# A planned order of 780 tasks, made anew: the combined weight w1·wo ahead of the first products of x, and the weight differences on VectorE alone

## The chip, the cores and the metric

The kernel runs on one core of one Trainium2 chip. The metric is the device time of one execution in microseconds (us). Five engines share the work: TensorE (PE in the profile, with PEld for its weight loads), VectorE (DVE), ScalarE (ACT), GpSimd (POOL) and SyncE (SP), which here issues nearly all DMAs. Each engine takes its instructions strictly in the order in which they are written, and waits where an input isn't there.

## The reference

```python
# q, k, v: (4, 8, 768, 64) float32; block 32, window 16, nb = 24
k_sum = k.reshape(B, H, nb, block, D).max(axis=3)
v_sum = v.reshape(B, H, nb, block, D).mean(axis=3)
scores_l = scale * q @ k^T,  kept where |i - j| < 16
scores_s = scale * q @ k_sum^T + log(block)
a = softmax(concat(scores_l, scores_s))
attn = a @ concat(v, v_sum)
x = attn.transpose(0, 2, 1, 3).reshape(3072, 512)
out = maximum(x @ w1, x @ w2) @ w_out      # w1, w2: (512, 1024), w_out: (1024, 512)
```

A local attention with block summaries is followed by a two-way maximum layer and an output product.

## The kernel before

The kernel uses max(x·w1, x·w2) = x·w1 + relu(x·(w2 - w1)). So it never forms x·w1: it multiplies w1·wo once into a 512x512 matrix (names w1o), and the output is x·w1o + relu(x·wd)·wo with wd = w2 - w1. Everything is computed in bf16 with float32 sums.

**Tiles.** The four batches are done one after the other. In each batch the 8 heads make 4 head pairs (hp 0 to 3), and the 768 rows make 3 groups of 256 (grp 0 to 2). Names carry these: k02 is the k block of batch 0, head pair 2; exp 021 is batch 0, head pairs 2 and 3, group 1; hidden 013 is batch 0, group 1, quarter 3.

**Steps of a batch.** k, q and v blocks (393 KB each) land in one of 13 float32 buffers (land), are cast to bf16 (kqb, vx), k and q are turned by PE (L624) or, in some late blocks, by a DMA transpose, and placed (kx, qx). For each pair of head pairs and each group PE makes the scores (L701), ACT the exponential (L715), DVE masks (L725, batches 1 to 3), PE multiplies with v and the block means (L757), DVE divides (L813, L816) into xs. xs is turned into xt by PE (L831, batch 0) or by a DMA transpose (L822, the other batches). Then follow four hidden products per group (L913, "hidden") with a relu each (L922 on ACT, L924 on DVE), and two output blocks (L940 with w1o, L947 with wo), copied and stored (L958).

**Weights.** w1 and w2 come as four tiles each (w0 to w3 in the plan's names), 0.52 MB, wo as four tiles as well. From each pair of tiles wd n = w2 - w1 is made (L856). The w1 tile is cast (w1b), turned by PE (L869, "turn w1") and copied out of PSUM (w1t). w1o takes 8 half blocks of 4 products on PE (L897): the first half of a block needs wo 0 and wo 1, the second wo 2 and wo 3. Their copies are the w1o tiles. Because a land buffer is freed only when its readers are done, a weight tile's buffer stays taken until both its cast and its wd are through.

**What sets the order.** The program is a list of 780 tasks, each with inputs, outputs and a choice of engines. Three tables fix the rest: `order` (in which order tasks are issued, hence each engine's queue), `engines` (a letter per task with a choice: T, D, A, P, S for PE, DVE, ACT, POOL, SP) and `slots` (which buffer of a ring each result takes).

```python
def given(self, order, slots):
    for t in order:
        for b in self.tasks[t].new:
            if b.slot is None:
                b.take(slots.pop(0))
        self.tasks[t].fn(self.tasks[t].letter)
```

Of the kernel before, what the change touches and what calls it, by code (L numbers as in the profile page):

```python
# [22 lines left out]
CFG = dict(  # L23
    kc="DAPA", qc="AAAA", kp="DDDD", qp="AADA", tl="DDDD", od="DDDD", se="AAAA", sr="PPPP", vc="PPPP",
    wd="PDDD", w1b="PPAD", w1t="DADD", wo="AADD", xt="AADDDD", kv=0.2, sp=0.7, ones=1, on="DDD", w=(30,
    31, 32, 33, 50, 51, 52, 53, 200, 201, 202, 203), wt=25, g0=(10, 30, 210), g1=(20, 30, 40), w1o=450, mx=1500,
    woc=600, wdp=30, lk="ADDP", lq="AAPA", lod="DPS", lse="DDD", lsr="DDP", lvc="DPPPDDAPPAPA", ltl="DDPD", ld=500, warm=14, cold=16500,
    turn="22 23 30 31 32 33", lx="SSS", cols=True, emb=1, ep=0.5, vt=0.28, s32=0.36, raw=0, qg=0, wh=1, os=6,
)
CFG["order"] = list(map(int, """  # L30
# [26 lines left out]
""".split()))  # L57
CFG["engines"] = "".join("""
PDPPPDDDPAPDPDDDDPTTTTTTTTTTTTTTSSSAAAATDDPPSSSADPATAAPPSSSPDDPTADDDSSSPDDPTADDPSSDPTASSPATDSSDATDSSPATASDSASASDDTDTAD
PPPDDTDTADPDADDTATDDPDDDPTATDDPPDDTTATDDTDTTATDDTDTTATDDTDTTATDDTDTTATDDTATTATDDTDSSSPSSSPSSSDSSSPPADAPDDDTAPDPAAPDPAT  # L60
DTDDADDDPTATDDPADDTADTDDSTADTDDSTADTDDSATPTADADADDTDTDDADAATADTDDSTADTDDSTADTDDSSSSPSSSASSSASSSPPDAPDDPPTDPPPAAAPPATDT
ADPAAAATPTADPPPDTADTDDSTADTDDSTADTDDSPSPSDDPAAASASDDPPPTADTDDSTADTDDSTADTDDSSSSPSSSPSSSASSSPPDAPDDPDTAPADPPPPPASPSDDAD
PDSDSDDPPDTADTDDSTADTDDSTADTDDSASPSADAADPSDSADAPDTADTDDSTADTDDSTADTDDSTTATTATTDTTDTDTATDTATTTDSTTTDSTATATATATTTAATTTAS
TATATDTDTTTASTTTDSTDTATDTDTTTDATTTDSTDTATATDTTTDATTTASTATDTATATTTDSTTTDSTATDTATATTTDATTTAATDTATATATTTASTTTASTATATATATT
TDSTTTAATDTDTDTDTTTDSTTTDATDTATDTDTTTDATTTASTATDTDTATTTAATTTDSTTTDSTTTAA
""".split())
CFG["slots"] = list(map(int, """
# [11 lines left out]
""".split()))  # L79
ENG = {"T": "PE", "D": "DVE", "A": "ACT", "P": "POOL", "S": "SP"}  # L80

# [153 lines left out]
def kernel(  # L235
# [15 lines left out]
    B, H, S, D = 4, 8, 768, 64  # L251
# [11 lines left out]
    op = plan.op  # L263
# [36 lines left out]
    wd = [Buf(Ring([wd_tile[:, n]])) for n in range(4)]  # L300
# [284 lines left out]
    def copy(engine, us, aps, label, port=True, by_engine=False, **kw):  # L585


        def fn(e):
            o, i = aps(e) if by_engine else aps()
            if e == "S":  # L590
                nc.sync.dma_start(out=o, in_=i)
            else:
                {"D": nc.vector.tensor_copy, "A": nc.scalar.copy, "P": nc.gpsimd.tensor_copy}[e](out=o, in_=i)  # L593

        op(engine, us, fn, label=label, port=port, **kw)

    def on(e):
        return {"D": nc.vector, "P": nc.gpsimd}[e]

    def prep(b, hp, prio, k_on, q_on, kp, qp, tail_on):  # L600
# [3 lines left out]
        for n, eng in enumerate((k_on,) if CFG["qg"] and b == 0 else (k_on, q_on)):  # L604
            by_dma = f"{b}{hp}" in CFG["turn"]
# [3 lines left out]
            def cast(e, f=f, src=src, n=n):  # L609
# [3 lines left out]
                if by_dma:  # L613
# [2 lines left out]
                return (src.ap[:].rearrange("p (i h d j) -> p h i j d", h=2, d=D, j=2),  # L616
                        landed(f, 2, J * D).rearrange("p h (i j d) -> p h i j d", d=D, j=2))

            copy(eng, {"D": 0.58, "A": 0.84 if by_dma else 1.06, "P": 0.83 if by_dma else 1.05}, cast, by_engine=True,
                 read=[f], write=[src], prio=prio, label=f"cast {'kq'[n]}{tag}")  # L620

            def turn(src=src, ps=ps):
# [223 lines left out]
    def load_w12(n, prios, prio, prio_t):  # L846
        rows, fs = n // 2, []
        h = half_of[n] // 2
        for w, at in zip((moe_w1, moe_w2), prios):
# [3 lines left out]
                out=landed(f, 2, 512), in_=w.rearrange("(c p) n -> p c n", p=128)[  # L853
                    :, 2 * rows:2 * rows + 2, 512 * h:512 * h + 512]),
               write=[f], prio=at, label=f"load w{n}")
        op(CFG["wd"][n], {"D": 1.23, "P": 2.35}, lambda e: on(e).tensor_tensor(  # L856
            out=wd_tile[:, 2 * h:2 * h + 2, 2 * rows:2 * rows + 2].rearrange("p n c f -> p c n f"),
            in0=landed(fs[1], 2, 512).rearrange("p c (n f) -> p c n f", f=256),
            in1=landed(fs[0], 2, 512).rearrange("p c (n f) -> p c n f", f=256), op=ALU.subtract),
# [145 lines left out]
    for n in range(4):  # L1005
        load_w12(n, CFG["w"][2 * n:2 * n + 2], CFG["wdp"] + 10 * n, CFG["wt"])
# [53 lines left out]
```

## Time and profile before

| | |
|---|---|
| median of 3 runs | 166.0 us (164.26 to 168.96) |
| the profiled execution | 166.2 us, of it 164.4 us span |
| TensorE busy | 153.0 us, 93% of the span |
| VectorE, ScalarE, GpSimd busy | 113.0, 92.9, 57.8 us |
| DMA | 36.46 MB, mean 222 GB/s |
| granted TensorE clock | 1.00 |

Rows of the profile name the line (L913), the engine, the operation, what it writes and reads (out<-in), how many instructions (x384), the busy time and the mean in ns of one, and the idle time before them with what ended it. A row of the timeline begins with the start and the length in us.

### The profile page before, as it was taken

What the parts mean: (1) busy time and instruction counts of PE and PEld (TensorE: products, weight loads), DVE (VectorE), ACT (ScalarE), POOL (GpSimd) and SP (SyncE); (2) the same over time, 40 slices, a digit from 0 to 9 for tenths busy, and PEclk for the clock granted to TensorE, in tenths of its full rate; (3) what the DMA queues carried; (4) which work ended last, traced back from release to release, by engine and by line L of the source; (5) the groups of instructions that cost most, each with busy time, mean ns of one, the idle gap of its engine ahead of it and who ended that gap; (6) DMA issues with size and microseconds to landing.
All of it is one profiled execution on the core that took longest, in us unless ns stands there. A gap on an engine that the chain in (4) does not pass through costs nothing.

```text
span 164.4 us, 4431 instructions
## 1 busy us (share of the span) xinstructions
PE 153.0 (93%) x1793; PEld 100.2 (61%) x1812; DVE 113.0 (69%) x224; ACT 92.9 (57%) x134; POOL 57.8 (35%) x91
## 2 busy tenths in 40 slices
PE   5889978999999999999999999999899999999992
PEld 2346657998565644575687646678545467766651
DVE  3698898579856899994989986569746654163221
ACT  3469995794577698836996645283937312012010
POOL 6058757302242385534672546034630000000000
PEclk9999999999999999999999999999999999999999
DMA  5999999999999999999979997997999996311015
GB/s 157 289 331 303 273 386 383 383 382 371 274 190 289 271 233 219 130 232 136 201 169 229 228 209 162 121 261 150 220 245 335 319 174 167 58 64 70 0 66 189
DMA packets 67700, 36.46 MB, mean 222 GB/s; under 512 B 54624, under 2 KB 61664, under 8 KB 67680
## 3 DMA queue, kind: packets, MB, share of 16 engines
q1 hardware_dynamic: 66208, 33.76, 87.6%
q10 hardware_dynamic: 1472, 2.43, 4.4%
q8 instruction: 14, 0.23, 0.6%
q14 instruction: 6, 0.05, 0.1%
HBM read 25.17 MB, written 6.29 MB: 191 GB/s over the span
## 4 chain that ended last, share of the span: by engine, by line
PE 62%; DMA 14%; DVE 11%; issue 4%; SPq 4%; ACT 2%; POOL 1%; ACTq 0%; POOLq 0%; DVEq 0%
PE banks L913 19%; PE banks L947 17%; PE banks L940 10%; DMA land<-in_k_dram 8%; DMA out_dram<-o 6%; PE banks L897 4%; PE banks L624 3%; PE banks L757 3%; DVE vx L593 3%; PE banks L701 2%; PE banks L982 2%; DVE ks L650 2%; DVE pb L725 2%; DVE kqb L593 1%; SPq L428 1%
## 5 line engine op out<-in xcount | busy, mean ns | idle before, releaser
L913 PE MATMUL banks<-xt,wd 128*128 128x256 bf16 x384 | 45.9, 273 | 0.1
L947 PE MATMUL banks<-wo,g 128*128 128x512 bf16 (+2 forms) x194 | 43.4, 362 | 1.8 <-issue 1.6
L913 PEld LDWEIGHTS <-wd 128*128 128x128 bf16 x384 | 37.3, 98 | 7.8 <-issue 0.5
L947 PEld LDWEIGHTS <-g 128*128 128x128 bf16 x208 | 18.7, 98 | 17.3
L715 ACT ACTIVATE pb<-banks 128x1024 bf16<-128x1024 f32 x24 | 23.6, 1026 | 6.2 <-PE banks L701 3.8
L940 PE MATMUL banks<-w1o,xt 128*128 128x512 bf16 (+2 forms) x100 | 23.5, 362 | 0.2
L922 ACT ACTIVATE g<-banks 128x512 bf16<-128x512 f32 x27 | 15.2, 604 | 7.6 <-PE banks L913 7.6
L924 DVE TENSOR_SCALAR g<-banks 128x512 bf16<-128x512 f32 x21 | 14.1, 686 | 7.8 <-PE banks L913 7.6
L816 DVE TENSOR_TENSOR xs<-banks,inv 128x512 bf16<-128x512 f32 x24 | 16.0, 686 | 4.9 <-DMA xt<-xs 4.4
L593 POOL COPY vx<-sums 32x792 bf16<-32x792 bf16 x15 | 14.7, 983 | 12.5 <-ACT sums L593 7.0
L725 DVE TENSOR_TENSOR pb<-pb,mask 128x1024 bf16<-128x1024 bf16 (+1 forms) x24 | 16.4, 710 | 4.0 <-ACT pb L715 3.7
L593 ACT COPY o<-banks 128x512 f32<-128x512 f32 (+1 forms) x8 | 4.4, 546 | 25.6 <-PE banks L947 21.1
L593 POOL CAST kqb<-land 128x768 bf16<-128x768 f32 x9 | 8.9, 985 | 20.1 <-DMA land<-in_q_dram 9.8
L940 PEld LDWEIGHTS <-xt 128*128 128x128 bf16 x104 | 9.9, 98 | 9.4
L650 DVE TENSOR_REDUCE ks<-kx 128x24 bf16<-128x768 bf16 x16 | 15.0, 945 | 0.2
L593 DVE COPY o<-banks 128x512 f32<-128x512 f32 (+2 forms) x10 | 6.2, 621 | 10.2 <-PE banks L947 8.7
L593 POOL CAST vx<-land 128x768 bf16<-128x768 f32 x10 | 8.9, 889 | 10.2 <-DMA land<-in_v_dram 10.2
L593 ACT CAST kqb<-land 128x768 bf16<-128x768 f32 x11 | 10.3, 943 | 3.2 <-DMA land<-in_k_dram 2.5
L593 DVE CAST kqb<-land 128x768 bf16<-128x768 f32 x12 | 7.0, 590 | 7.1 <-DMA land<-in_k_dram 4.7
L624 PE MATMUL banks<-ident,kqb 128*128 128x128 f32 x60 | 9.7, 278 | 1.4 <-DVE kqb L593 1.1
L757 PEld LDWEIGHTS <-pb 128*64 128x64 bf16 (+1 forms) x384 | 8.0, 110 | 4.9 <-issue 2.8
L757 PE MATMUL banks<-vx,pb 128*64 128x65 bf16 (+1 forms) x384 | 9.5, 196 | 1.3 <-DVE xs L816 0.8
(87 smaller groups left out, 183.1 us busy)
## 6 DMA issues: line engine op xcount, KB each, us to landing
land<-in_k_dram SPq DMA_DIRECT2D x16, 384.0 KB, 6.0
land<-in_v_dram SPq DMA_DIRECT2D x16, 384.0 KB, 6.9
land<-in_q_dram SPq DMA_DIRECT2D x16, 384.0 KB, 5.9
land<-in_moe_w_dram SPq DMA_DIRECT2D x8, 512.0 KB, 9.6
land<-in_moe_w_out_dram SPq DMA_DIRECT2D x4, 512.0 KB, 10.0
out_dram<-o SPq DMA_DIRECT2D x7, 256.0 KB, 4.0
out_dram<-o ACTq DMA_DIRECT2D x4, 256.0 KB, 2.8
out_dram<-w1t SPq DMA_DIRECT2D x3, 256.0 KB, 3.4
```

What stands on the lines that cost most here:

```text
L593: {"D": nc.vector.tensor_copy, "A": nc.scalar.copy, "P": nc.gpsimd.tensor_copy}[e](out=o, in_=i)
L624: nc.tensor.transpose(out=bank(ps)[:, 128 * j:128 * j + 128], in_=src.ap[:].bitcast(F32)[:, 128 * j:128 * j + 128], identity=ident32[:])
L650: op("D", 0.95, lambda e: nc.vector.tensor_reduce(out=ks.ap[:, 0:nb], in_=free(kt(), 128, [256, NM], [192, 2], [32, 2], [1, 32]), axis=AX. ...
L715: op("A", {"A": 1.03}, lambda e: nc.scalar.activation(out=spread(pb.ap[:, 0, 0:1], [192, 8], [128, 2], [1, 64]) if PW > 128 else spread(pb ...
L725: nc.vector.tensor_tensor(out=o, in0=o, in1=spread(mask[:, 2 * u:2 * u + 1, 0:1], [0, n], [64, 2], [1, 64]), op=ALU.mult)
L757: nc.tensor.matmul(out=o, lhsT=p[r], rhs=vx[b].ap[r, par, hp + n, 2 * grp + u, a, 0:D + 1], start=(PW == 128 or par == 0), stop=(last and ...
L816: op("D", 0.69, lambda e: nc.vector.tensor_tensor(out=x.ap[:].rearrange("p n u a d -> p n (u a) d"), in0=spread(bank_tile[:, ps.ap, 0:1], ...
L913: nc.tensor.matmul(out=bank(ps)[:, 256 * s:256 * s + 256], lhsT=wd_tile[:, quarter, c, 128 * s:128 * s + 128], rhs=x.ap[:, c, :], start=(c ...
L922: nc.scalar.activation(out=o, in_=bank(ps), func=ACT.Relu)
L924: nc.vector.tensor_scalar_max(out=o, in0=bank(ps), scalar1=0.0)
L940: nc.tensor.matmul(out=bank(ps, c1 - c0), lhsT=x.ap[:, c, sl], rhs=w1o[c].ap[:, cols], start=(c == 0), stop=False)
L947: nc.tensor.matmul(out=bank(ps, c1 - c0), lhsT=g.ap[:, f, sl], rhs=wo[f // 2].ap[:, f % 2, cols], start=False, stop=(f == FC - 1))
```

## The change

Three things change. The three tables are replaced by others: `order`, `engines` and `slots`. The task wd loses its choice of engine, so all four run on DVE, where before wd 1 and wd 3 ran on POOL. And the planner's cost of an ACT cast of k and q goes from 1.06 to 1.0, a number that a fixed order does not read.

```diff
 CFG["order"] = list(map(int, """
-44 32 2 0 3 10 12 1 4 6 11 15 13 8 112 20 30 26 56 25 46 113 116 9 122 7 123 126 14 47 16 117 34 118 132 168 28 23 133
...
+2 32 112 10 15 44 122 18 26 113 24 34 3 16 123 21 68 56 46 116 70 45 4 1 9 126 128 117 6 7 35 142 132 127 12 118 119 8
...
-            copy(eng, {"D": 0.58, "A": 0.84 if by_dma else 1.06, "P": 0.83 if by_dma else 1.05}, cast, by_engine=True,
+            copy(eng, {"D": 0.58, "A": 0.84 if by_dma else 1.0, "P": 0.83 if by_dma else 1.05}, cast, by_engine=True,
...
-        op(CFG["wd"][n], {"D": 1.23, "P": 2.35}, lambda e: on(e).tensor_tensor(
+        op("D", {"D": 1.23}, lambda e: on(e).tensor_tensor(
```

PE keeps its 239 tasks. DVE has 213 tasks instead of 210, ACT 156 instead of 143, POOL 71 instead of 82, SP 101 instead of 106. Five stores move from SP's queue to ACT's.

**SP, the loads from the 14th on.** in_moe_w rows are halves of a pair of w1 and w2 tiles (512 KB), in_moe_w_out rows are wo. The first twelve loads were all of batch 0; in the new order the first thirteen hold these and one k block of batch 1 (k12). Before:

```order
L852 DMA land_62<-in_moe_w_dram 128x2x512
L852 DMA land_63<-in_moe_w_dram 128x2x512
L852 DMA land_64<-in_moe_w_dram 128x2x512
L428 DMA land_66<-in_k_dram 128x2x384
L852 DMA land_67<-in_moe_w_dram 128x2x512
L852 DMA land_68<-in_moe_w_dram 128x2x512
L428 DMA land_69<-in_k_dram 128x2x384
L852 DMA land_71<-in_moe_w_dram 128x2x512
L852 DMA land_72<-in_moe_w_dram 128x2x512
L883 DMA land_73<-in_moe_w_out_dram 128x2x512
L428 DMA land_70<-in_k_dram 128x2x384
L428 DMA land_74<-in_k_dram 128x2x384
```

Now:

```order
L852 DMA land_70<-in_moe_w_dram 128x2x512
L428 DMA land_62<-in_k_dram 128x2x384
L852 DMA land_63<-in_moe_w_dram 128x2x512
L852 DMA land_67<-in_moe_w_dram 128x2x512
L883 DMA land_68<-in_moe_w_out_dram 128x2x512
L883 DMA land_71<-in_moe_w_out_dram 128x2x512
L883 DMA land_72<-in_moe_w_out_dram 128x2x512
L852 DMA land_64<-in_moe_w_dram 128x2x512
L883 DMA land_66<-in_moe_w_out_dram 128x2x512
L852 DMA land_73<-in_moe_w_dram 128x2x512
L852 DMA land_69<-in_moe_w_dram 128x2x512
L428 DMA land_74<-in_k_dram 128x2x384
```

Before, each tile's w1 and w2 came one behind the other and wo as the 23rd and 26th to 28th load. Now the four w1 tiles are the 14th, 16th, 17th and 21st load (w1, w3, w2, w0), wo 1, wo 0, wo 2 and wo 3 the 18th, 19th, 20th and 22nd, and the w2 tiles, which only wd reads, the 23rd, 24th, 26th and 27th. The first twelve change as well: q00 was the 8th load behind two v blocks, and is the 9th behind three.

**PE, the start of the big blocks.** Before, behind the last turn of xs and the turn of a k block, PE begins hidden (L913):

```order
L831 LDWEIGHTS xs_109
L831 MATMUL banks<-identity,xs_109 128x128
L624 MATMUL banks<-ident_139,kqb_75 128x128 x3
L913 LDWEIGHTS wd
L913 MATMUL banks<-xt_113,wd 128x256
```

Now, behind a turn of xs (x 022), it begins w1o (L897):

```order
L831 LDWEIGHTS xs_110
L831 MATMUL banks<-identity,xs_110 128x128
L897 LDWEIGHTS w1t_125
L897 MATMUL banks<-wo_130,w1t_125 128x512
L897 LDWEIGHTS w1t_125
```

Seven of the eight halves of w1o, the last turn of w1 and three turns of xs now stand between there and the first hidden; before, the eight halves came behind eleven hidden blocks. wo_130 is wo 0.

**DVE, from the second-last group's division to wd.** Before, DVE did two of the four wd behind the first relu (g):

```order
L593 COPY w1t_125<-banks 128x4x256
L924 TENSOR_SCALAR g_120<-banks 128x512
L856 TENSOR_TENSOR wd<-land_71,land_68 128x2x2x256
L856 TENSOR_TENSOR wd<-land_72,land_67 128x2x2x256
L593 COPY kx_80<-banks 128x6x2x64
```

Now the casts of wo 0 and w1b 0 stand among the divisions, and wd 1 and wd 3 ahead of any relu:

```order
L593 CAST wo_130<-land_71 128x1024
L593 COPY kx_80<-banks 128x6x2x64
L813 RECIPROCAL inv_143<-banks 128x8
L816 TENSOR_TENSOR xs_110<-banks,inv_143 128x512
L593 COPY xt_114<-banks 128x512
L593 CAST w1b_123<-land_64 128x1024
L816 TENSOR_TENSOR xs_111<-banks,inv_143 128x512
L650 TENSOR_REDUCE ks_100<-kx_79 128x24
L593 COPY xt_115<-banks 128x512
L856 TENSOR_TENSOR wd<-land_73,land_70 128x2x2x256
L856 TENSOR_TENSOR wd<-land_69,land_63 128x2x2x256
```

(A second RECIPROCAL row, ahead of the w1b cast, is left out.) Behind them follow a maximum of k (L650), a relu, a small copy, and wd 0 and wd 2. On POOL, the casts of wo 2, wo 3, a w1 tile and blocks of k and q of batch 1 stand where its two wd stood. On ACT, the last three exponentials of batch 0 now come behind the cast of a w1 tile and of a k block, and the copies of q from PSUM, which DVE did, are ahead of the first.

More of the change, by code (lines that the diff above doesn't have):

```diff
@@ L30 @@
 CFG["order"] = list(map(int, """
[26 rows of a table removed]
[26 rows of a table added]
 """.split()))
 CFG["engines"] = "".join("""
[L59 to L65, printed above, removed]
+DDDDDPPPPDPDDPDPDPTTTTTTTTTTTTTTSSSPAPPTDDDDSSSDPAATADDDSSSADPATAAPPSSSDADATADDDSSDDTASSDATDSSDPTASSDPTDSDSASPSPDTDTAD
+AADADTPTDDAAAAPTDTDDPDDDATDTDDPPDDTTATDDTATTATDDTDTTATDDTATTATDDTATTATDDTDTTATDDTDSSSPSSSDSSSPSSSPDDDPPDPPTDDAPADPDPPT
+DTDDDPDDPTPTADAPDATADTDDSTADTDDSTADTDDSATPTDDPADDPTDTDDADDDTADTDDSTADTDDSTADTDDSSSSASSSASSSPSSSADDPPPADPTDDPADPPPADTAT
+DDAPPDDTATDDAADDTADTDDSTADTDDSTADTDDSPSPSDDDDPPSASADAPPTADTDDSTADTDDSTADTDDSSSSDSSSPSSSDSSSADPDDDADPTDAAPAPDPAPSDSADAP
+DPSDSDDDDATADTDDSTADTDDSTADTDDSPSDSDDDPPASASADDAATADTDDSTADTDDSTADTDDSTTATTATTATTATATATDTATTTDSTTTASTATATATDTTTAATTTAA
+TDTATATATTTASTTTDATATDTATDTTTASTTTASTATDTATATTTDSTTTDATATATATATTTDATTTAATATDTDTATTTASTTTASTATATDTATTTAATTTAATATDTATATT
+TAATTTAATATATATATTTAATTTASTDTDTDTATTTDATTTAATATDTDTATTTDSTTTDATTTAATTTDS
 """.split())
 CFG["slots"] = list(map(int, """
[11 rows of a table removed]
[11 rows of a table added]
 """.split()))
```

72 rows, old and new, of the table turn are left out of this document.

## The prediction

> **What bounds the kernel now.** I read the page first, for the busiest engine and for where it idles.
>
> ```profile
> span 164.4 us, 4431 instructions
> PE 153.0 (93%) x1793; PEld 100.2 (61%) x1812; DVE 113.0 (69%) x224; ACT 92.9 (57%) x134; POOL 57.8 (35%) x91
> PE   5889978999999999999999999999899999999992
> PE 62%; DMA 14%; DVE 11%; issue 4%; SPq 4%; ACT 2%; POOL 1%; ACTq 0%; POOLq 0%; DVEq 0%
> ```
>
> TensorE (PE) is the bound, and a change of order removes no PE instruction. Its holes lie in the first slices. So I asked for busy times by stage, cut where the chain of work changes: first transpose, last warm-up product, end of the first attention, first w1o product, last product.
>
> ```profile
> 0.00:5.89 5.89, 3.55 (x9) 1.07 (x9) 2.24 (x9) 1.28 (x1) 2.81 (x16) 1.00 0.68 220
> 5.89:15.64 9.75, 9.00 (x57) 5.12 (x58) 8.37 (x25) 7.70 (x14) 5.49 (x10) 1.00 1.18 305
> 15.64:28.72 13.08, 11.06 (x297) 8.31 (x297) 11.45 (x31) 10.59 (x13) 9.40 (x11) 1.00 1.10 339
> 28.72:40.27 11.55, 11.55 (x114) 10.52 (x115) 8.48 (x15) 8.78 (x14) 2.40 (x3) 1.00 1.05 382
> 40.27:161.20 120.93, 117.89 (x1322) 75.14 (x1338) 82.20 (x149) 64.50 (x93) 37.69 (x52) 1.00 0.90 189
> 161.20:164.39 3.19, 0.00 (x0) 0.00 (x0) 0.28 (x1) 0.03 (x1) 0.00 (x0) 1.00 0.50 168
> ```
>
> The first number behind the stretch is its length, the second PE's busy time; the last three are granted clock, DMA share and GB/s. From 28.72 on PE idles 3.04 us of 132.5. Between 15.64 and 28.72 it idles 2.02 us, and before that it mostly runs warm-up products that compute nothing. So the kernel ends when it does because dense useful work begins at about 29 us; a later beginning moves the end by as much, and an earlier one can bring 2 us plus part of the 3. The DMA share is above 1 from 5.89 to 40.27: loads land as fast as the engines carry them, and their order decides what is there. The chain of waits says what set the beginning:
>
> ```profile
> 17.55 10.09 DMA land<-in_k_dram
> ...
> 27.67 1.01 ACT kqb L593
> ...
> 28.72 0.55 PE banks L624 x3
> 29.27 2.62 PE banks L913 x24
> ```
>
> A k block lands at 27.64, is cast and turned, and behind that turn stands the first product with wd. From there PE does not stop.
>
> **The change part by part.** The sum is made against the profiled execution, 166.2 us (span 164.4 and 1.8 around it); the runs have their median at 166.0.
>
> First, what PE must have done when the first big block starts. Before, that block is hidden (L913), and after, it is w1o (L897). Ahead of w1o stand one w1 turn and one k turn more than stood ahead of hidden, and three turns of x fewer. Prices:
>
> ```profile
> 27.92 0.68 PE L831 MATMUL banks<-identity,xs 128*128 128x128 bf16 x9 [0.66 <-issue]
> 29.11 0.60 PE L913 MATMUL banks<-xt,wd 128*128 128x256 bf16 x4
> 31.89 0.45 PE banks L869 x8
> 33.66 0.33 PE banks L624 x3
> 42.48 3.45 PE banks L897 x16
> 65.83 0.45 PE banks L757 x16
> ```
>
> A w1 turn is 0.45, a k turn 0.33, a turn of x about 0.22 (4 of such 9), a hidden block (8 products) a third of the 2.62 above, 0.87, half a w1o block (4 products) 0.86, a head group's values 0.45. The difference is 0.45+0.33-0.66 = +0.12 us of work already done. Before, the first hidden product starts at 29.11; if w1o starts at 29.11+0.12 = 29.2, PE is level with before; each us later is a us lost.
>
> When can w1o start? It needs wo 0 and wo 1. In the new order wo 0 is the 19th load, the second w0 tile's first half (w1 of w0) the 21st, the last operand of wd 3 the 24th, of wd 2 the 27th. Twelve loads of q, k, v and nearly the same mix of half-MB weights stand ahead of these places in both orders, so the n-th load should land when the n-th did. These instructions of before start as a load lands:
>
> ```profile
> 29.08 1.04 ACT L593 CAST w1b<-land 128x1024 bf16<-128x1024 f32 x1 [0.41 <-DMA land<-in_moe_w_dram]
> 30.39 1.04 POOL L593 CAST w1b<-land 128x1024 bf16<-128x1024 f32 x1 [2.55 <-DMA land<-in_moe_w_dram]
> 32.77 2.52 DVE L856 TENSOR_TENSOR wd<-land,land 128x1024 bf16<-128x1024 f32 x2 [1.90 <-DMA land<-in_moe_w_dram]
> 36.53 0.61 DVE L593 CAST kqb<-land 128x768 bf16<-128x768 f32 x1 [0.78 <-DMA land<-in_k_dram]
> 37.51 0.99 POOL L593 CAST kqb<-land 128x768 bf16<-128x768 f32 x1 [5.71 <-DMA land<-in_k_dram]
> 38.81 0.69 DVE L593 CAST wo<-land 128x1024 bf16<-128x1024 f32 x1 [0.25 <-DMA land<-in_moe_w_out_dram]
> ```
>
> They are the 18th, 19th, 21st, 24th, 25th and 26th load. So wo 0 lands at about 30.3; VectorE (DVE) casts it in 0.69 (last row), and w1o starts at 31.0 instead of 29.2: **+1.8 us**. The lower bound is the first attention itself, if the loads come sooner. Its last exponential is later too. Its q block of the first pair is the 9th load instead of the 8th with one v block more ahead, 0.393 MB at the 305 GB/s of that stage, 1.3 us. Before, ScalarE (ACT) ran thus:
>
> ```profile
> 11.01 0.26 ACT L593 CAST apart<-banks 64x128 bf16<-64x128 f32 x1 [1.31 <-PE banks L523]
> 14.32 0.29 ACT L593 COPY vx<-vx 32x128 bf16<-32x128 bf16 x1
> 16.54 2.86 ACT L715 ACTIVATE pb<-banks 128x1024 bf16<-128x1024 f32 x3
> 21.95 1.04 ACT L593 CAST w1b<-land 128x1024 bf16<-128x1024 f32 x1
> ```
>
> 16.54+1.3 = 17.8 is when its first exponential could start in the new order. From there it has six exponentials (5.7), two sums (0.5), a small copy (0.3), and between them a w1b, a k cast and a v cast (about 1 each, 2.9); a sum and two copies that now stand ahead of the first I count half, 0.4. That is 9.8, to 27.6. With the last values, a k turn, a w1 turn and one turn of x PE reaches w1o at 29.05: -0.2. The upper bound is +3.0: GpSimd's (POOL's) sums for the last head group come behind its casts of a k block and of w1b 3, and each can push by its 1 us.
>
> Second, wd on DVE alone. It frees POOL of two instructions and gives DVE two:
>
> ```profile
> L856 POOL TENSOR_TENSOR wd<-land,land 128x1024 bf16<-128x1024 f32 x2 | 4.7, 2358 | 0.3 <-DMA land<-in_k_dram 0.2
> L856 DVE TENSOR_TENSOR wd<-land,land 128x1024 bf16<-128x1024 f32 x2 | 2.5, 1226 | 2.0 <-DMA land<-in_moe_w_dram 1.9
> L593 POOL CAST kqb<-land 128x768 bf16<-128x768 f32 x9 | 8.9, 985 | 20.1 <-DMA land<-in_q_dram 9.8 <-DMA land<-in_k_dram 9.6 <-POOL vx L593 0.6
> ```
>
> After 31.0 PE has seven halves of w1o (6.0), a w1 turn and three turns of x (1.1), and wants the first hidden block at 38.2. Its w1 turn needs w1b 0: 21st load 32.7, cast 0.69, 33.4, while PE comes there at 31.0+2.6 = 33.6. wd 3 has its last operand at 36.5 and is done at 37.75, 0.4 us early. Queued behind it on DVE are a maximum (0.95), the first relu (0.69), a small copy (0.25) and wd 0 and wd 2 (2.45); the relu waits for the first hidden block at 39.1, so wd 2 is done at 42.5, and PE wants it after four hidden blocks, a turn and a w1o half, at 42.9. Both have 0.4 us in hand, and POOL's casts of k11 and q12 run beside them. What two DVE operands cost beside POOL, one row shows:
>
> ```profile
> 92.52 1.90 DVE L725 TENSOR_TENSOR pb<-pb,mask 128x512 bf16<-128x512 bf16 x2
> ...
> 92.36 0.83 POOL L593 CAST vx<-land 128x768 bf16<-128x768 f32 x1 [1.74 <-DMA land<-in_v_dram]
> 93.13 1.02 POOL L593 CAST kqb<-land 128x768 bf16<-128x768 f32 x1
> ```
>
> Two half masks took 1.90 us beside two POOL casts. Their shortest, by the mask line, is 0.41 each:
>
> ```profile
> L725 DVE TENSOR_TENSOR pb<-pb,mask x24: 412/680/1421, 53.0 to 130.5; 128x1024 bf16<-128x1024 bf16 x12, 128x512 bf16<-128x512 bf16 x12
> ```
>
> So about 1 us can be added, one POOL cast. Less the 0.4 in hand and at even odds, I take **+0.2**, bounds 0 and +1.4. The Trainium skill's "SBUF — State Buffer", section "Who interferes with whom", says that a VectorE instruction with two SBUF inputs shares a read port with GpSimd, and the later of the two is blocked outright. That speaks against wd on DVE; wd has two such inputs. The 1.90 us agrees with it. By the rule alone each wd that meets a cast pays its 0.99 whole.
>
> Third, the rest. After its first 40 us PE has the same work. The products of w1o no longer follow hidden; they stand ahead of it, which costs nothing by itself. The tightest place I find is late: between the last values of x block 300 and its hidden stand 5.2 us of PE work (five blocks of 0.87 and two values). Ahead of it DVE needs an inverse and a product, 0.88, and the transposing DMA its 4.2:
>
> ```profile
> L816 DVE TENSOR_TENSOR xs<-banks,inv 128x512 bf16<-128x512 f32 x24 | 16.0, 686 | 4.9 <-DMA xt<-xs 4.4
> L813 DVE RECIPROCAL inv<-banks 128x8 f32<-128x8 f32 x24 | 4.2, 191 | 5.5 <-PE banks L757 5.4
> xt<-xs SPq DMA_TRANSPOSE x18, 4.2
> ```
>
> That is 5.1 against 5.2. I take **+0.3** for the whole rest, with -1.0 (a third of the 3.04 us idle) and +1.5 as bounds. Stores move from SyncE's to ACT's queue; both engines idle there, so nothing is added.
>
> Sum: 166.2+1.8+0.2+0.3 = **168.5 us**, 1.5% above the median.
>
> **The rivals.**
>
> (1) DVE becomes the gate. Place: its queue from wo 0 to wd 2. For it: it runs in order, it gains 2.45 us there, and POOL casts wo 2, wo 3, k11, q12, q11 at the same time. Against it: before, its wd ran at 1226 both times, with POOL idle. If wd 1 and wd 3 each wait for one cast, wd 3 ends at 37.75+2*0.99 = 39.7, and hidden starts 1.5 after PE could begin it: this 1.5 in place of the 0.2 gives 169.8. It decides from 0.4 us of delay on, and passes 2% at 1.4. The Trainium skill's rule above makes it so wherever a cast is under way first.
>
> (2) Loads are hidden. If wo 0 lands by 28.5, w1o starts at 29.0 by ACT's chain: 166.2-0.2+0.2+0.3 = 166.5. For it: the weights that wd alone needs now come last. Against it: DMA share above 1 throughout.
>
> (3) The longer distance pays. Between an x block of the first batch and its hidden now lie 8 to 12 us of PE work instead of 3 to 5.5. If all 2.02 us of holes before 28.72 go and a third of the later ones, 166.2-2.0-1.0 = 163.2. Against it: wo 0 still lands at 30.3.
>
> **How the numbers follow.** Forecast 0.50, rival (1) 0.32, rival (2) 0.12, rival (3) 0.06. About 2% is what a measurement of this kernel can tell from no change, here 162.7 to 169.3. Of the forecast's share some 0.08 lies above 169.3 (w1o later than 31.5), and of rival (1) all but 0.02; rival (3) gives up 0.01 to the middle. So slower 0.38, faster 0.05, within 2% 0.57. The range 165.4 to 171.4 runs from below rival (2) to a delay of 3.0 at w1o with the other two terms at about 1; it leaves out rival (3) and some late stalls.
>
> **What would show it.** In the profile after, w1o (L897) should begin near 31.0, with PE idle in the 4 us ahead of it, and the DVE cast of wo 0 should start as a load ends. Hidden (L913) should follow near 38.2, wd near 1.23 us each. A wd near 2.2, or PE waiting for DVE L856, is rival (1). w1o at 29 or sooner proves the first term wrong. PE idling over 4.5 us between 42 and the end proves the third wrong, as does a chain of waits that leads there through an xt transpose.

## The result: 2.9% slower, inside the range, for another reason than forecast

The change takes 170.12 us (median of 4 runs, 169.93 to 170.72), the kernel before 165.64 beside it (164.26 to 168.96): a ratio of 1.0285, 95% interval 1.0235 to 1.0334. Executions more than 1.5% above the fastest of the same kernel are left out of every ratio here, so a ratio can differ a little from the quotient of two medians. The forecast was 168.5, the range 165.4 to 171.4.

The page of the profiled execution (170.02 us) begins thus: span, busy times, the row of PE's 40 slices, and the chain of work that ended last.

```profile
span 168.2 us, 4465 instructions
...
PE 157.0 (93%) x1812; PEld 100.8 (60%) x1812; DVE 112.9 (67%) x224; ACT 96.3 (57%) x142; POOL 57.8 (34%) x83
...
PE   4897988999999988899999999999999999999993
...
PE 75%; DVE 14%; DMA 4%; issue 2%; SPq 2%; ACT 2%; POOL 1%; DVEq 0%; POOLq 0%
```

The chain's DMA share fell from 14% to 4%, nearly all of it one k block at the start, and PE's rose; so behind that block hardly a load ends a wait of the chain. The two profiled executions differ by 3.8 us, less than the medians, since that of before was slower than its median. Where the 3.8 us of span went is seen by cutting both traces where the big blocks begin and where the last product ends. First before, from hidden on; then the change, from w1o on, and its tail (length first, then PE's busy time).

```profile
29.11:161.20 132.09, 129.05 (x1432) 85.28 (x1448) 90.29 (x161) 73.25 (x107) 40.09 (x55) 1.00 0.91 205
```

```profile
32.09:165.37 133.28, 130.79 (x1453) 85.03 (x1450) 87.74 (x162) 75.62 (x110) 40.77 (x49) 1.00 0.87 193
165.37:168.21 2.84, 0.00 (x0) 0.00 (x0) 0.33 (x2) 0.00 (x0) 0.00 (x0) 0.91 0.54 180
```

The big blocks begin 2.98 us later; with the 0.12 of work done by then, 2.86 are lost. From there to the last product the change needs 133.28 instead of 132.09: with the same 0.12, 1.31 more. The tail is 0.35 shorter than the 3.19 of before. Together 3.8. PE's own rows show both places.

```profile
31.41 0.62 PE L869 MATMUL banks<-identity,w1b 128*128 128x128 bf16 x8 [0.27 <-issue]
...
32.09 2.75 PE L897 MATMUL banks<-wo,w1t 128*128 128x512 bf16 x12
...
36.66 2.75 PE L897 MATMUL banks<-wo,w1t 128*128 128x512 bf16 x12
39.25 1.91 PE L913 MATMUL banks<-xt,wd 128*128 128x256 bf16 x16
...
44.50 1.70 PE L913 MATMUL banks<-xt,wd 128*128 128x256 bf16 x14 [0.19 <-DVE wd L856]
...
62.27 0.68 PE L701 MATMUL banks<-qx,kx 64*128 64x64 bf16 x36 [0.68 <-DVE kx L593]
...
67.11 0.78 PE L757 MATMUL banks<-vx,pb 128*64 128x65 bf16 x16 [0.79 <-DVE o L593]
68.30 0.45 PE L757 MATMUL banks<-vx,pb 128*64 128x65 bf16 x16 [0.41 <-DVE pb L725]
```

w1o starts at 32.1, hidden at 39.25, neither with a wait just ahead of it; wd 2 costs 0.19; and between 62 and 69 us PE waits three times for DVE, 1.88 in all. The casts of wo 0 (DVE) and wo 2 (POOL) tell whether loads were late.

```profile
29.96 1.04 POOL L593 CAST wo<-land 128x1024 bf16<-128x1024 f32 x1 [0.49 <-DMA land<-in_moe_w_out_dram]
...
30.70 0.85 DVE L593 CAST wo<-land 128x1024 bf16<-128x1024 f32 x1
```

POOL's cast of wo 2, the 20th load, starts as that load ends, at 29.9. wo 0 is the 19th, so it landed earlier still, and DVE took it up at 30.7 only when its queue came to it, without idle time ahead. The forecast had wo 0 land at 30.3 and DVE wait for it.

### The profile page after: what moved, and what is told of

Read it like the earlier page. It is cut to its first block, busy times and chain, and to the rows that moved or that the text cites. A ratio compares the mean times of both kernels' runs of the same rounds, so it can differ in the third digit from the quotient of the medians.

```text
span 168.2 us, 4465 instructions
## 1 busy us (share of the span) xinstructions
PE 157.0 (93%) x1812; PEld 100.8 (60%) x1812; DVE 112.9 (67%) x224; ACT 96.3 (57%) x142; POOL 57.8 (34%) x83
## 4 chain that ended last, share of the span: by engine, by line
PE 75%; DVE 14%; DMA 4%; issue 2%; SPq 2%; ACT 2%; POOL 1%; DVEq 0%; POOLq 0%
PE banks L913 23%; PE banks L947 23%; PE banks L940 10%; PE banks L757 4%; PE banks L897 4%; DMA land<-in_k_dram 4%; PE banks L701 3%; PE banks L624 3%; DVE pb L725 3%; DVE vx L593 3%; DVE wd L856 2%; DVE kx L593 2%; SPq L428 1%; PE banks L869 1%; ACT qx L593 1%
## 5 line engine op out<-in xcount | busy, mean ns | idle before, releaser
L947 PE MATMUL banks<-wo,g 128*128 128x512 bf16 (+2 forms) x208 | 46.3, 363 | 0.0
L913 PE MATMUL banks<-xt,wd 128*128 128x256 bf16 x384 | 45.2, 273 | 0.2 <-DVE wd L856 0.2
L913 PEld LDWEIGHTS <-wd 128*128 128x128 bf16 x384 | 37.3, 98 | 7.5 <-DVE wd L856 0.5
L922 ACT ACTIVATE g<-banks 128x512 bf16<-128x512 f32 x33 | 18.7, 600 | 18.2 <-PE banks L913 18.1
L593 POOL CAST kqb<-land 128x768 bf16<-128x768 f32 x13 | 14.9, 1153 | 30.8 <-DMA land<-in_q_dram 9.7
L924 DVE TENSOR_SCALAR g<-banks 128x512 bf16<-128x512 f32 x15 | 10.3, 690 | 20.5 <-PE banks L913 20.5
L593 ACT COPY o<-banks 128x512 f32<-128x512 f32 (+1 forms) x12 | 6.6, 560 | 17.7 <-PE banks L947 17.6
L650 DVE TENSOR_REDUCE ks<-kx 128x24 bf16<-128x768 bf16 x16 | 14.9, 943 | 0.1
L982 PE MATMUL banks<-identity 128*128 128x512 bf16 x28 | 10.3, 487 | 1.6 <-DVE ks L344 1.6
L624 PEld LDWEIGHTS banks<-ident,kqb 128*128 128x128 f32 x60 | 7.8, 153 | 6.8 <-POOL apart L368 2.1
L593 POOL COPY vx<-sums 32x792 bf16<-32x792 bf16 x10 | 9.4, 938 | 5.9 <-DVE sums L593 3.4
L701 PEld LDWEIGHTS <-kx 64*128 64x128 bf16 x416 | 7.0, 94 | 7.3 <-issue 5.7
L593 DVE CAST kqb<-land 128x768 bf16<-128x768 f32 x12 | 8.9, 751 | 3.6 <-DMA land<-in_k_dram 2.9
```

What stands on the lines that cost most here:

```text
L624: nc.tensor.transpose(out=bank(ps)[:, 128 * j:128 * j + 128], in_=src.ap[:].bitcast(F32)[:, 128 * j:128 * j + 128], identity=ident32[:])
L650: op("D", 0.95, lambda e: nc.vector.tensor_reduce(out=ks.ap[:, 0:nb], in_=free(kt(), 128, [256, NM], [192, 2], [32, 2], [1, 32]), axis=AX. ...
L701: nc.tensor.matmul(out=bank(ps, second=a)[:, at + n0:at + n1], lhsT=kx[b, hp + n].ap[r, 128 * t + 128:128 * t + 256], rhs=q_of(n, r, c, c ...
L913: nc.tensor.matmul(out=bank(ps)[:, 256 * s:256 * s + 256], lhsT=wd_tile[:, quarter, c, 128 * s:128 * s + 128], rhs=x.ap[:, c, :], start=(c ...
L922: nc.scalar.activation(out=o, in_=bank(ps), func=ACT.Relu)
L947: nc.tensor.matmul(out=bank(ps, c1 - c0), lhsT=g.ap[:, f, sl], rhs=wo[f // 2].ap[:, f % 2, cols], start=False, stop=(f == FC - 1))
```

## The experiments

Two theories stood at the start. F: the first attention is late, by engine queues, and sets w1o. W: wd on DVE beside POOL's casts sets hidden (rival 1 of the prediction). Kernels made from the change have their line numbers 7 higher (a w1 turn is L876, w1o L904, hidden L920, wd L863, mask L732). In the diffs, "engines" and "order" lines stand for entries of those tables.

**wd back on POOL**

```diff
-        op("D", {"D": 1.23}, lambda e: on(e).tensor_tensor(
+        op(CFG["wd"][n], {"D": 1.23, "P": 2.35}, lambda e: on(e).tensor_tensor(
-engines: wd 1, wd 3: D
+engines: wd 1, wd 3: P       order: both ahead of POOL's cast k11
```

> The changed kernel with wd 1 and wd 3 back on POOL, ahead of its cast of k11; all else as changed. Theory F (the first attention is late, PE reaches w1o at 32.1 and would be at hidden at 39.2 whatever wd does): w1o stays at 32.1, hidden at 39.2 to 39.4 (POOL ends wd 3 near 39), time 170.1 within 0.5. Theory W (rival 1 of the prediction: wd on DVE beside POOL's casts sets the end): hidden comes 1 to 1.5 us earlier or the time falls by that much, to about 168.6.

Measured: 170.76 us, ratio 1.029 (1.0215 to 1.0366); w1o at 31.9, hidden at 39.1. That part of the change, undone, brings nothing.

**No POOL cast beside wd**

```diff
-engines: cast k11, q12, q11, k10: P
+engines: cast k11, q12: A   cast q11, k10: D
+order: k11, q12 behind ACT's first two copies of w1o; q11, k10 behind wd 2; max k13 behind wd 3
```

> The changed kernel with no POOL cast beside wd: the casts of k11 and q12 on ACT, those of q11 and k10 on DVE behind wd 2, and DVE's maximum of k13 behind wd 3. All four wd should take 1.2 us. Theory F: wd 3 is done near 37.4, but PE comes to hidden only at 39.2, so only the wait of 0.2 at wd 2 goes: 169.9. Theory W: hidden starts up to 1.8 us earlier and the time is about 168.3.

Measured: 169.87 us, ratio 1.0238 (1.0151 to 1.0324). The groups of instructions (count, busy time, mean ns of one): wd and POOL's casts of k and q in the change, then wd here.

```profile
L856 DVE TENSOR_TENSOR wd<-land,land 128x1024 bf16<-128x1024 f32 x4 | 6.3, 1610 | 0.0
...
L593 POOL CAST kqb<-land 128x768 bf16<-128x768 f32 x13 | 14.9, 1153 | 30.8 <-DMA land<-in_q_dram 9.7
```

```profile
L863 DVE TENSOR_TENSOR wd<-land,land 128x1024 bf16<-128x1024 f32 x4 | 4.7, 1218 | 0.0
```

So the casts did stretch wd, and without them each takes 1.22. Yet hidden begins at 39.05 instead of 39.25, and the median falls by 0.3, about the price that F gave it. wd was slow behind cover. W falls as the cause.

**The first attention, and both edits together**

```diff
-engines: place q00: A
+engines: place q00: D       order: DVE's copy odd v040 behind x 002
```

> The changed kernel with two edits in the first attention: block q00 is copied out of the bank by DVE instead of by ACT behind q01, and DVE's copy odd v040 stands behind x 002 instead of ahead of x 001. Theory F: the first exponential starts near 18.4 instead of 19.2, PE reaches w1o near 31.0 instead of 32.1; hidden then has to wait for wd 3, which ends at 39.2 as before the edit, so hidden stays near 39.2 and the time near 170.0, with PE idle about 1 us ahead of hidden. Theory L (the prediction's: the loads and the cast of wo 0 set w1o): w1o stays at 32.1 and nothing moves. If wd were no gate at all: hidden near 38.2 and 169.0.

The second run here has this edit and that of the run before.

> Both edits together: the first attention as in the run with q00 and odd v040 moved, wd as in the run without POOL casts beside it. If both gates stand one behind the other (F, then W): w1o near 31.0, hidden near 38.1, time 168.8 (1.3 less than the change), though each edit alone brings 0.2 at most. If only F holds: the same as the front edit alone would then be about 169.0. If the loss lies elsewhere (late stalls alone): 170 in all of these runs.

Measured: 170.53 (1.028, 1.0205 to 1.0356) and 170.03 us (1.0244, 1.0172 to 1.0317). w1o at 32.0 and 32.2, hidden at 39.2 and 39.7. The last exponential ended at 29.97 and 29.55 instead of 30.16, but w1o did not follow. So F falls too, as far as it names engine queues. What took up the time gained is a wait ahead of a w1 turn. The sooner the last exponential ended (30.16, 29.97, 29.55, and 29.28 without POOL casts beside wd), the longer PE idles there: 0.27 us in the change, then 0.41, 0.89 and 0.91. With wd back on POOL it ended at 30.37, and no idle time shows. In the run without POOL casts beside wd:

```profile
29.70 0.55 PE L631 MATMUL banks<-ident,kqb 128*128 128x128 f32 x3
31.16 0.62 PE L876 MATMUL banks<-identity,w1b 128*128 128x128 bf16 x8 [0.91 <-DVE inv L820]
```

The turn needs w1b 2, which POOL had cast by 29.4, and a bank that DVE had read by 29.9. PE stands until 31.16 all the same; the releaser printed there is merely the last event that came before. The stages up to this instant show what it has in common with the wait of 0.66 in the kernel before, at 27.92 (the second number of each engine is its count, PE and PEld first):

```profile
0.00:27.91 27.91, 22.93 (x351) 13.99 (x351) 21.76 (x62) 18.81 (x27) 17.69 (x36) 1.00 1.04 301
```

```profile
0.00:31.40 31.40, 25.56 (x350) 15.12 (x350) 24.13 (x60) 20.41 (x31) 17.01 (x34) 1.00 1.04 316
```

```profile
0.00:31.49 31.49, 25.31 (x350) 14.74 (x350) 23.38 (x63) 19.82 (x31) 16.89 (x34) 1.00 1.02 311
```

Before, the change, and the kernel with both edits: PE stands after 702, 700 and 700 of its instructions, at 27.9, 31.4 and 31.5 us, before at a turn of x and in the other two at a w1 turn. These views leave out PE's semaphore waits. With them 705 recorded instructions stand ahead of the wait in each of the three. PE idles at the same count, 0.4 to 1.2 us, in every other trace here without added products, but for the one with wd on POOL. A wait at a fixed count points to the code. The DMA view has a queue of kind "instruction"; in the change, first cut to the two hundredths of a microsecond from 28.98, then whole (packets begun, MB, share of 16 engines' time; the packet takes longer than that cut).

```profile
q8 instruction: 1, 0.02, 341.2%
```

```profile
q8 instruction: 14, 0.23, 0.6%
```

14 packets of 16 KB for PE's 3624 products and weight loads are some 259 instructions in each; the table takes 256, which the next experiment tests. From the start times in the traces (us; a page is what one packet brings, a boundary the instruction 256 ahead of the wait):

| kernel | PE passes a boundary | the next page's packet begins | PE goes on |
|---|---|---|---|
| before | 21.72 | 25.45 | 27.92 |
| the change | 25.14 | 28.99 | 31.41 |
| wd on POOL | 25.01 | 28.80 | 31.21 |
| no casts beside wd | 24.92 | 28.70 | 31.16 |
| both edits | 25.24 | 28.96 | 31.50 |

The page begins 3.7 to 3.9 us after a boundary and PE goes on 2.4 to 2.5 us later: 6.2 to 6.3 us for 256 instructions, whatever is ready. In that stretch the first attention's small products would use them up faster. From before to the change the boundary is passed 3.42 us later, and PE goes on 3.49 later.

**The test of the code theory: 160 instructions more, and 256**

```diff
+            few = n in (0, 2, 3, 6, 8, 9, 10, 13)       # warm-up groups
-            for _ in range(2):
+            for _ in range(1 if few else 2):             # products of 512 columns
+            for _ in range(11 if few else 0):            # 17 in the control: products of 32 columns
```

> The kernel with both edits of the first attention and of wd, and in eight of the early warm-up groups one product of 512 columns replaced by eleven of 32 columns: 160 PE instructions more, which compute nothing, before the first transpose of q. Code theory: PE's instructions come in pages of 256 by a DMA queue of their own; PE stands at its 705th instruction in every run so far, whatever is ready, because the page that begins there is there only 2.4 us after its transfer begins. The pages then begin 160 instructions earlier in the program, where PE has time: the wait of 0.9 ahead of the w1 turn goes, w1o starts near 31.2 instead of 32.2, hidden near 38.7 instead of 39.7, time 169.1 instead of 170.0. Rival (the wait is for data or a bank that the profile does not name): nothing moves, w1o at 32.2, 170.0.

> The control for the kernel with 160 more PE instructions: seventeen small products in place of eleven, 256 instructions more, so the pages begin at the same places of the program as without any. Code theory: the wait of 0.9 ahead of the w1 turn is back, w1o near 32.2, hidden near 39.7, time 170.0. Rival (the small products help or hurt for another reason, the clock or PE's early queue): the same as with 160.

Measured: 170.78 us (1.0331, 1.0151 to 1.051) and 170.81 us (1.036, 1.0288 to 1.0432). The w1 turn and the k turn ahead of it, with 160 and then with 256, and there the stage up to the wait:

```profile
32.61 0.55 PE L631 MATMUL banks<-ident,kqb 128*128 128x128 f32 x3
32.99 0.61 PE L876 MATMUL banks<-identity,w1b 128*128 128x128 bf16 x8
```

```profile
31.50 0.55 PE L631 MATMUL banks<-ident,kqb 128*128 128x128 f32 x3
32.64 0.62 PE L876 MATMUL banks<-identity,w1b 128*128 128x128 bf16 x8 [0.59 <-POOL wo L600]
```

```profile
0.00:32.63 32.63, 26.98 (x478) 17.35 (x478) 24.80 (x61) 19.92 (x31) 16.91 (x34) 1.00 1.02 306
```

With 160 it is gone, with 256 it is back, after 956 instructions: 700 + 256. There is one packet more in both (15). The theory of the wait is shown. Its size is seen from the first scores to w1o: 13.05 us with 160, 14.30 with 256, 13.92 with neither. The time did not fall, since both kernels start their scores late, at 20.6 and 19.0 instead of 18.3. q00 landed at 15.3 and 16.6 there, instead of 15.1. With 160, PE's other products ahead of the scores also took longer than without: a group of six block sums 0.82 us instead of 0.50, and a pair of products of 512 columns 1.05 instead of 0.59.

```profile
13.15 0.82 PE L530 MATMUL banks<-vx,amean 128*128 128x128 bf16 x6
13.76 1.05 PE L697 MATMUL banks<-hide,identity 128*128 128x512 bf16 x2
```

```profile
12.07 0.50 PE L530 MATMUL banks<-vx,amean 128*128 128x128 bf16 x6
12.41 0.59 PE L697 MATMUL banks<-hide,identity 128*128 128x512 bf16 x2
```

So the small products did not replace the large ones without loss. Which of these made the scores late is not settled.

**The late waits**

```diff
-engines: copy out 000: D     cast k23, cast v22: P
+engines: copy out 000, cast k23, cast v22: A      order: all three behind exp 102
```

> The changed kernel with three instructions at 63 to 67 us moved to ACT, behind its exponential of 102: the copy of the first output block (before on DVE, 0.69) and the casts of k23 and v22 (before on POOL, beside DVE's mask of 122, which took 1.91). Theory: PE waited 0.79 and 0.41 there for DVE's queue and 0.68 for a sum of k10 just before; without POOL beside it the mask takes 0.7 to 1.3, the two waits of 1.2 go and the first stays: 1.2 us less than the change, 168.9. Rival (the waits only move, since PE is held by something further on): 170 within 0.5.

Measured: 168.52 us (1.0235, 1.0189 to 1.0281). DVE's and POOL's rows there in the change, and DVE's mask in this run:

```profile
63.51 0.84 POOL L593 CAST kqb<-land 128x768 bf16<-128x768 f32 x1
63.68 1.91 DVE L725 TENSOR_TENSOR pb<-pb,mask 128x512 bf16<-128x512 bf16 x2
64.30 1.01 POOL L593 CAST vx<-land 128x768 bf16<-128x768 f32 x1
```

```profile
64.29 0.76 DVE L732 TENSOR_TENSOR pb<-pb,mask 128x512 bf16<-128x512 bf16 x2
```

Two half masks take 1.91 us beside POOL's two casts and 0.76 without. Of PE's three waits only the first (0.68) is left, and from hidden to the last product it takes 1.3 us less; in the median, 1.6. Expected were 1.2. This is the change's second loss. Contention explains 1.15 us of DVE's time there; the edit also took a copy of 0.69 out of DVE's queue, and no run separates the two.

**Everything together, with and without the code edit.** In the kernel with it, eight warm-up groups have twelve products of 32 columns and none of 512.

> The kernel with no POOL cast beside wd, and the three instructions at 63 to 67 us on ACT. If the two add up: 0.3 and 1.5 us below the change, 168.4; w1o still near 31.9 with the wait for PE's code ahead of it.

> The kernel with all edits so far that helped (no POOL cast beside wd, and the three instructions at 63 to 67 us on ACT), and in eight warm-up groups both products of 512 columns replaced by twelve of 32: 160 PE instructions more, without PE time more. Code theory: no wait at the w1 turn; w1o near 31.1 instead of 31.9, hidden near 38.3, time 0.7 below the same kernel without them (167.7 against 168.4). Rival: the same time and the same wait as without them.

Measured: without, 168.28 us (1.0209, 1.012 to 1.0299), the sum of the two gains (0.3 and 1.6) as expected. With it, 167.72, 168.95, 169.61 and 186.37 us (1.0257, 1.0135 to 1.0378). The rows without and with it:

```profile
29.90 0.55 PE L631 MATMUL banks<-ident,kqb 128*128 128x128 f32 x3
31.41 0.62 PE L876 MATMUL banks<-identity,w1b 128*128 128x128 bf16 x8 [0.97 <-DVE inv L820]
```

```profile
30.78 0.55 PE L631 MATMUL banks<-ident,kqb 128*128 128x128 f32 x3
31.16 0.61 PE L876 MATMUL banks<-identity,w1b 128*128 128x128 bf16 x8
31.83 1.46 PE L904 MATMUL banks<-wo,w1t 128*128 128x512 bf16 x5
```

The wait is gone again: from the first scores to w1o PE needs 12.65 us instead of 13.58. But q00 landed at 16.3 instead of 15.2 in that execution and the scores began 0.7 later, so hidden gained 0.6 and the runs do not tell the two apart. Why q00 landed later is open. No version here beats the kernel before.

**What makes the first scores late**

```diff
 the kernel with both edits:
+order: load v03 behind load q00; DVE's cast q00 ahead of max k02 and cast v03; what needs v03, and v02, later on PE, DVE, ACT
-engines: w1b 1, cast k12: A
+engines: w1b 1, cast k12: P
```

> The kernel with both edits, and the first attention turned towards its q block: q01 and q00 load ahead of v03, DVE casts q00 ahead of v03, what needs v03 comes later on PE, DVE and ACT, ACT's casts of w1b 1 and k12 go to POOL, which idles then. Theory (the 2.06 us by which q00 lands later in the change is the loss, carried to w1o by PE's code pages): PE passes its 193rd instruction about 1.5 us earlier than at 19.7, so w1o starts near 30.6 and hidden near 38.1, time 168.5. Rival (the weights' loads and casts hold w1o and hidden anyway): the exponentials come earlier, w1o stays at 31.8 to 32.2, 170.

Measured: 170.15 us (1.0339, 1.0252 to 1.0427). q00 landed at 13.6, 1.4 sooner, but the scores began at 18.46: PE's queue now stood at the block sums of v03, which the edit had made late, and at two warm-up groups behind them. So this run moved the load and not the scores, and decides nothing on them; w1o began at 33.0. The reverse was tried on the kernel before:

```diff
 the kernel before:
-order: load q01 ... load q00 ... load v02, load v03
+order: load v02, load v03, load q01 ... load q00
```

> The kernel before, with one edit: the loads of v02 and v03 stand ahead of those of q01 and q00 instead of behind, so q00 lands about 2.3 us later (15.3), nearly as in the change (15.0). Nothing of wd, w1, wo or their order is touched. Theory (the first scores come late, and PE's code pages carry that to the first big block one for one): the first scores start near 18.3 instead of 16.1, PE's 705th instruction and hidden come about 2.3 us later (hidden near 31.4 instead of 29.1), time 2 to 2.4 us above the kernel before. Rival (hidden waits for the 17th load, k12, and its chain, which lands as before): hidden at 29.1 to 29.7, time at most 0.6 above.

Measured: 171.08, 171.60, 204.24 and 546.14 us; the first two give a ratio of 1.0382 (1.026 to 1.0503). The rival allowed 0.6. The sizes cannot be taken from its profile, that of the 204.24 us, with a granted clock of 0.76; there q00 landed 4.1 us later, more than the 2.3 expected, and k03, whose load stands between q01 and q00, was late as well. So the rival is out, as far as two executions tell, and q00, q01 and k03 landing late cost the kernel before as much as the whole change does. That the loss is one for one is not shown.

**wd on DVE alone, in the kernel before**

```diff
 the kernel before:
-engines: wd 1, wd 3: P
+engines: wd 1, wd 3: D
```

> The kernel before with one part of the change alone: wd 1 and wd 3 on DVE, at the place in the order where POOL had them. POOL is idle beside them, so each takes 1.2. DVE has 0.6 us of idle time between 24 and 29, and all of x stands in its queue there: the two would delay the turns of x by 2.4 less 0.6, hidden to 30.9 and the time by 1.8. If PE's code and k12 hold hidden until 28.7 anyway and half of the delay is hidden: 1.0. If wd on DVE costs nothing even here: the same as before within 0.5.

Measured: 166.80 us, ratio 1.0114 (1.0039 to 1.019), about 2 us; each wd 1.22, hidden at 30.75 after 29.11, and PE waited 0.55 ahead of it for wd. Not all of the 1.64 is wd's, though. In this execution PE already met a wait for code one page (256 instructions) sooner, ahead of DVE's first wd at 26.47:

```profile
22.98 0.44 PE L759 MATMUL banks<-vx,pb 128*64 128x65 bf16 x15 [0.88 <-issue]
```

So it passed that boundary at 22.98 instead of 21.72, and went on behind the next page at 29.18 instead of 27.92. What the trace gives to wd is the 0.55, on the way to the first big block. In the change wd stands behind w1o and costs 0.2.

## Why the prediction was right, and where it was not

**Right:** the sign, the range, the place of the main loss, and the way from w1o to hidden (7.2 us forecast and measured). Term 1 said that the time is decided by when PE can start its first big block, and that w1o would come late: 1.8 us were taken, with bounds of -0.2 and +3.0, and 2.9 were measured. That it fell inside its bounds is in part luck, since the loss came by another path.

**The cause of term 1 was wrong.** The step "the n-th load should land when the n-th did" failed: the 19th load, wo 0, landed at 28.55 and not at 30.3, even the 20th by 29.9, and nothing waited for wo 0. The named sign (DVE's cast of wo 0 starts as a load ends) did not appear. The bound by ACT's chain, 27.6 for the last exponential, also failed: it ended at 30.2. It rested on q00 being 1.3 us later; it landed at 15.0 after 12.95, 2.06 later (a v block lands 1.7 to 1.8 us behind the load ahead of it, where the mean rate gave 1.3), and its way to the first scores was 0.3 longer. So the scores came 2.3 us later, and w1o 13.70 us behind them, where hidden came 13.05 behind them before. The first exponential started at 19.17 instead of 17.8, and the six took 11.0 instead of 9.8, with two of them waiting for PE. Ahead of w1o PE's code sets a floor of 6.2 us for each 256 instructions, which kept up to 0.9 us from being made up (13.05 instead of 13.92, and 12.65 instead of 13.58, where its wait was taken away). In the change itself attention and code were late together, since PE idles only 0.27 at that place. That q00's landing makes the loss is read from the traces; the run that landed it sooner did not test it.

**A row was read for its price alone.** The row of 27.92 in the prediction ends in "[0.66 <-issue]". It was used for the price of a turn of x; the wait was the one for code. It did not set hidden's start in the kernel before: the turns behind it ended at 28.60, and PE's next, the k turn at 28.72, followed the cast of k12, as the prediction says. But it stood close behind that gate, and in the change the same wait stands on the way to w1o.

**Term 2 had the right size.** Taken were 0.2 us; PE waited 0.19 for wd 2. That wait and a wd near 2.2 were the named signs of rival (1), and both showed, the second nearly: the shortest and longest wd took 1.21 and 2.01, where 1.23 and at worst a cast of 0.99 more was assumed. The Trainium skill, "SBUF — State Buffer", section "Who interferes with whom", says that the port pair shared by VectorE and GpSimd is an exclusive lock and that issue order decides who blocks. The trace agrees in both directions: POOL's three casts of k and q beside wd took 1.56, 2.07 and 1.98 us, where the one just ahead of them took 0.99, and without them wd is at 1218 ns again. Still rival (1) was not the cause. Rival (1) priced this at 1.5 us at hidden. The two runs on wd show 0.3 at most there, since PE itself came to hidden only at 39.2.

**Term 3 was too small.** Taken were 0.3; net of before it was 1.1 (the 1.31 less the 0.19 at wd 2). At the place named, xt 300, PE did not wait. The loss sits at 62 to 69 us, where rival (1)'s mechanism is seen at another place, DVE's masks beside POOL's casts. Its lower bound was a misreading too: of the 3.04 us in which PE seemed idle after 28.72, much is products missing from the record. The groups of the output products, before and after:

```profile
L947 PE MATMUL banks<-wo,g 128*128 128x512 bf16 (+2 forms) x194 | 43.4, 362 | 1.8 <-issue 1.6
```

```profile
L947 PE MATMUL banks<-wo,g 128*128 128x512 bf16 (+2 forms) x208 | 46.3, 363 | 0.0
```

The order changes no product, so both kernels have 208 of them. 14 are not recorded before, and 1.8 us of "idle" stand ahead of those that are. The kernel before was denser than it looked, which leaves rival (3) less to win. The sign set for this term, 4.5 us of idle PE behind 42 us, came from the same number and so meant nothing.

**Rival (2)** had its condition met but for 0.05 us: by the record of its transfer wo 0 landed at 28.55, where 28.5 was asked. Still w1o did not start at 29.0, since its bound, ACT's chain, was the wrong one.

## What to carry to other kernels

When an engine stands and what the profile names as its releaser was done long before, count its instructions up to the wait, in several runs: a wait that stays at a count and not at a piece of work was one for code here, and work that was ready sooner only made it longer. Instructions added to move the pages have a price of their own: with them the products ahead of the scores ran slower. Price a contended instruction where its cover ends: wd stretched by up to 0.8 us cost 0.2 ahead of a late PE, and masks stretched by 1.15 stood ahead of waits of 1.2 where PE had no cover. And compare the count of a group with what the program issues before calling a gap idle.

## What was not expected of the hardware

PE's code arrives in packets of 16 KB, 256 instructions each, on a DMA queue of its own. With the DMA share above 1 around it, a page began 3.7 to 3.9 us after PE passed the boundary ahead of it, in the five kernels of the table; later in the change it was 0.4 (77.54 to 77.97) to 3.0 us. Whether the loads make the difference was not tested. 160 instructions that compute nothing (80 small products more, with their weight loads), placed early, moved the pages and took a wait of 0.9 us away, though not the time.
